# Linear-attention numerators as 64x32 tiles of TensorE, two PSUM banks a chunk, and a new table of offsets

## The chip, the cores and the metric

The kernel runs on one core of one Trainium2 chip. The metric is the device time of one execution in microseconds. Engines are named as in the profile: PE (TensorE, with PEld for its weight loads), DVE (VectorE), ACT (ScalarE), POOL (GpSimd), SP (the queue that issues DMAs).

## The reference, cut to what matters

Two attention layers are computed and laid side by side in the output. The first (A: four segments with a compressive memory) is not touched by the code of the change, only by the order of the work. The second (B) is a linear attention over 2048 tokens, 32 heads of 32 dimensions, 64 features a head:

```python
qkv = (x @ wqkv)                       # q, k, v: 32 heads of 32
pq = einsum("bhsd,hdf->bhsf", q, w_phi); pk = einsum("bhsd,hdf->bhsf", k, w_phi)
phi_q = concat([softmax(pq), softmax(-pq)]); phi_k = concat([softmax(pk), softmax(-pk)])
kv = einsum("bhsf,bhsd->bhfd", phi_k, v)      # 64 x 32 for each head
z = einsum("bhsf->bhf", phi_k)
num = einsum("bhqf,bhfd->bhqd", phi_q, kv)    # the numerators
den = einsum("bhqf,bhf->bhq", phi_q, z)[..., None] + 1e-6
out = (num / den).reshape(B, S, D) @ wo
```

## The kernel before, in words

All products run in float16 with each operand split into a high and a low half, so that a product is three matmuls: high by high, high by low, low by high (the pairs `(0, 0), (0, 1), (1, 0)` in the code).

The program is a list of operations, each with an engine, a planned duration and a priority. `Graph.run` is a planner: it walks through planned time, takes on each engine the ready operation of the smallest priority number, gives each PSUM tile one of eight banks at its first use, and emits the instructions in that order. Operations that follow one another with the same priority form a job, numbered through the program; the table `MOVES` adds an offset to the priority of a job on one engine, so a negative number draws that job's work on that engine ahead. Counted through the program, job 284 holds the last sums of `kv`, 285 the spreading of `z`, 287 the scaling and splitting of `kva` into `kls`, 291 to 298 and 303 to 310 the first two query products with their evictions (292, 294, 296, 298, 304, 306, 308 and 310 those of the evictions), 298 and 301 also the chains of the first two chunks, 299 the first projection with its stores, 340 a part of A's weights; after 390 come A's output products.

In time, the first half of the span is A's attention (to some 920 us), then B's values and states `kv` (to some 1215 us), then B's queries in 16 chunks of 128 tokens, then A's output projection (line 1666). The change lies in B's queries. Every second chunk a query product for 256 tokens is made (`strassen`, line 608, three or four banks), and `expo` (lines 1262 to 1275) makes of it the two softmaxes' exponentials `e`. For each chunk and each half `hb` of the heads POOL and DVE work out the denominators (lines 1578 to 1589) and scale `e` (line 1591), ACT and DVE split it into float16 halves `eh` (lines 1598 and 1600), and a transposing DMA on SP makes `pt`: features on partitions, two heads (2 x 64 features) in each of 8 groups (line 1603).

`kls` holds for each pair of heads a block of 128 features by 64 columns (2 heads x 32 dimensions). It is block diagonal: `bm2` has set the two quarters to zero in which one head's features meet the other's dimensions. The numerators of one half (line 1612, function `f`) are 4 x 3 x 2 = 24 matmuls over 128 partitions with 64 columns of weights and 128 tokens, two column tiles by turns, into one bank of the kind "pv". ACT then writes the high half of `ot` (line 1616) and DVE the low half (line 1618), for this half of the heads. When all of `ot` is there, `project` multiplies it by `wo` (48 matmuls of 512 columns a chunk, line 394 with `ot`), and the result goes out.

Of the kernel before, what the change touches and what calls it, by code (L numbers as in the profile page):

```python
# [12 lines left out]
AF = mybir.ActivationFunctionType  # L13
OP = mybir.AluOpType
# [5 lines left out]
D = 1024  # L20
# [34 lines left out]
         ((3, 0, "subtract"), 3, 2), ((2, 3, "subtract"), 2, 6))  # L55
EUP = 2.0 ** 15
MOVES = {
    "DVE": {
# [3 lines left out]
    "ACT": {  # L62
# [9 lines left out]
    "POOL": {  # L72
        67: 17, 70: -1, 93: -6, 131: -0.5, 141: 1, 148: -7.5, 199: 13.5, 217: -4, 238: -38, 245: 0.5, 250: -4.5, 312: -5},
    "SP": {
        88: 5.5, 89: 3.5, 134: 33.5, 149: -3.5, 226: -19.5},
}


# [20 lines left out]
class Graph:  # L99
# [84 lines left out]
    def run(self):  # L184
# [3 lines left out]
        banks, used = [[0.0, None, ()] for _ in range(8)], {k: 0 for k in self.KEEP}  # L188
        never = float("inf")
# [7 lines left out]
            if not o.wait:  # L197
                lists[o.eng].append(o)

        def bank(kind):  # L200
            rest = [x for x in banks if x[1] is None]
            if used[kind] >= self.MOST[kind] or len(rest) <= sum(
                    max(0, n - used[k]) for k, n in self.KEEP.items() if k != kind):
                return never, None
            return min((x[0], i) for i, x in enumerate(banks) if x[1] is None)

        def start(o):
            t = max(o.ready, held["POOL" if o.eng == "DVE" else "DVE"]) if o.port else o.ready
            for b in o.banks:
                if b.at is None:  # L210
                    t = max(t, bank(b.kind)[0])
            return t

        def safe(o):

            return max([o.safe] + [bank(b.kind)[0] + self.SLACK for b in o.banks if b.at is None])

        count = 0
        for _ in self.ops:
# [60 lines left out]
def tile_kernel(ctx: ExitStack, tc: tile.TileContext, ax, aw, awv, awo, beta, bx, bwqk, bwv, bphi, bwo, out):  # L280
# [93 lines left out]
    def bank(tag, shape, line=None):  # L374
        b = G.bank(tag, shape, F32, line or tag)
        psums.add(b)
        return b
# [105 lines left out]
    def rows(v, n):  # L483
        return v.rearrange("p c n -> p (c n)") if n == 1 else v.rearrange("p (a c) n -> p a (c n)", a=n)
# [1060 lines left out]
    for c in range(NT):  # L1545
# [24 lines left out]
        def otv(ot=ot):  # L1570
            return ot()[:, 0:2048].rearrange("p (a g t) -> p a g t", a=2, g=NG)

        for hb in range(2):
            e, r = er[c % 2, hb]
            dn = G.buf("b", [128, 16, 2], F32, "dn", 2)
# [21 lines left out]
            for q in range(2):  # L1597
# [5 lines left out]
            op(SP, 2.9, lambda pt=pt, hv=hv: nc.sync.dma_start_transpose(  # L1603
                pt().rearrange("p a g t -> p (a g) t"), hv().rearrange("p a n -> p (a n)")),
               r=[(eh, (hb, a, q)) for a in range(2) for q in range(2)], w=[pt], prio=P, lat=1.2, kb=64)
            pn = bank("pv", [128, 4, 128])

            def f(pn=pn, pt=pt, hb=hb):
                for g in range(4):
                    for a, b in ((0, 0), (0, 1), (1, 0)):  # L1610
                        for k in range(2):
                            nc.tensor.matmul(pn()[64 * k:64 * k + 64, g, :], kls()[:, a, 8 * hb + 2 * g + k, :], pt()[:, b, 2 * g + k, :],  # L1612
                                             start=(a + b == 0), stop=(a == 1), skip_group_check=True)

            op(PE, 0.85, f, r=[(kls, (0, hb)), (kls, (1, hb)), pt], w=[pn], prio=P)
            op(ACT, 0.55, lambda pn=pn, hb=hb, otv=otv: nc.scalar.activation(
                otv()[:, 0, 4 * hb:4 * hb + 4, :], pn(), AF.Copy, scale=2.0 ** -15), r=[pn], w=[(ot, (0, hb))], prio=P)
            op(DVE, 0.62, lambda pn=pn, hb=hb, otv=otv: nc.vector.scalar_tensor_tensor(  # L1618
                otv()[:, 1, 4 * hb:4 * hb + 4, :], pn(), 2.0 ** -15, otv()[:, 0, 4 * hb:4 * hb + 4, :], op0=OP.mult, op1=OP.subtract),
               r=[pn, (ot, (0, hb))], w=[(ot, (1, hb))], prio=P)  # L1620
        project(lambda a, g: (ot, None, lambda otv=otv: otv()[:, a, g, :]), bo, c * 128, 1024, P + 1.1)


# [114 lines left out]
```

## Time and profile before

| | |
|---|---|
| median of 3 runs | 1698.13 us (1698.09 to 1698.71) |
| the profiled execution, its own time | 1699.08 us |
| its span in the trace | 1697.4 us |
| mean granted clock of TensorE | 0.994 |
| busy: PE, DVE, ACT, POOL | 98%, 80%, 68%, 57% |
| numerators on PE (line 1612) | 768 matmuls in 32 blocks, 27.5 us busy |

The span runs from the first to the last instruction; the execution's own time has 1.7 us more around it. Busy time counts an instruction from its start to its end, and matmuls overlap, so a block's cost is read from starts, not from summed durations.

### The profile page before, as it was taken

The numbers are of one execution on the slowest core, as the hardware profiler recorded it, in microseconds if no ns is written. First come the engines' busy times: TensorE is split into PE (matmuls) and PEld (weight loads), VectorE is DVE, ScalarE is ACT, GpSimd is POOL, SyncE is SP. The second block draws the span as 40 slices with busy tenths as digits, with TensorE's granted clock in tenths as the row PEclk, the third lists the DMA queues.
The fourth block names the chain that finished last, engine by engine and source line by source line (L and its number), as shares of the span: only waits on it lengthen the run. The fifth ranks groups of instructions, "written<-read, shape, count | busy, mean of one in ns | idle before, by whom it ended". The sixth has DMA issues, their size and how long they took to land.

```text
span 1697.4 us, 38668 instructions
## 1 busy us (share of the span) xinstructions
PE 1668.2 (98%) x14408; PEld 1002.5 (59%) x14408; DVE 1354.2 (80%) x3205; ACT 1158.9 (68%) x2131; POOL 965.4 (57%) x1280
## 2 busy tenths in 40 slices
PE   8999999999999999999999999999999999999999
PEld 6677676766767767767765455445544444444444
DVE  5889998899988869698895779677998887975441
ACT  8788899878879797868675477765545644544331
POOL 3346588554468885848552577645488887640000
PEclk8999999999999999999999999999999999999999
DMA  5556465755776665764467465467645876773311
GB/s 192 165 183 176 139 206 175 242 160 163 225 179 204 184 173 150 199 189 131 95 182 266 156 224 162 137 194 278 224 94 149 199 162 174 214 168 129 124 62 62
DMA packets 261933, 292.47 MB, mean 172 GB/s; under 512 B 138865, under 2 KB 192881, under 8 KB 255089
## 3 DMA queue, kind: packets, MB, share of 16 engines
q1 hardware_dynamic: 261744, 290.01, 57.3%
q8 instruction: 113, 1.85, 0.5%
q14 instruction: 76, 0.61, 0.1%
HBM read 161.17 MB, written 86.05 MB: 146 GB/s over the span
## 4 chain that ended last, share of the span: by engine, by line
PE 45%; DVE 5%; DMA 1%; ACT 0%; issue 0%; SPq 0%; DVEq 0%; ACTq 0%
PE proj L608 17%; PE misc L394 8%; PE proj L1666 5%; PE s L608 4%; PE s L1666 2%; PE misc L608 2%; PE kv L1423 1%; PE misc L1666 1%; PE pv L1612 1%; DVE S L1600 1%; PE proj L394 1%; DVE mx L1262 1%; DVE r L1272 1%; DVE dn L1581 1%; PE pv L1007 1%; PE s L971 1%
## 5 line engine op out<-in xcount | busy, mean ns | idle before, releaser
L394 PE MATMUL proj<-S,S 128*128 128x128 f16 (+1 forms) x3072 | 508.8, 301 | 4.1 <-ACT S L427 1.7
L394 PEld LDWEIGHTS <-S 128*128 128x128 f16 x4608 | 330.2, 98 | 152.0 <-issue 13.0
L608 PE MATMUL proj<-S,S 128*128 128x512 f16 x1584 | 364.6, 379 | 2.4 <-ACT cs L614 2.4
L608 PEld LDWEIGHTS <-S 128*128 128x128 f16 x2016 | 191.9, 98 | 220.5 <-issue 3.3
L984 POOL TENSOR_SCALAR_AFFINE_SELECT ph<-ph 128x256 f16<-128x256 f16 (+1 forms) x448 | 195.8, 458 | 155.2 <-DVE ph L978 136.7
L876 DVE CUSTOM_DVE_ANT_0 s<-s,causal 128x512 f32<-128x512 f32 (+3 forms) x512 | 242.9, 509 | 15.2 <-PE s L870 11.5
L978 DVE SCALAR_TENSOR_TENSOR ph<-s,ph 128x512 f16<-128x512 f32 x320 | 210.2, 683 | 36.8 <-ACT ph L977 35.3
L977 ACT ACTIVATE ph<-s 128x512 f16<-128x512 f32 x320 | 189.9, 653 | 1.0 <-PE pv L1007 0.2
L394 PE MATMUL misc<-S,ot 128*128 128x512 f16 x768 | 170.8, 379 | 1.8 <-DVE ot L1618 1.8
L1269 ACT ACTIVATE e<-e,sk 128x256 f32<-128x256 f32 x256 | 113.3, 497 | 63.7 <-DVE e L1266 58.2
L394 PEld LDWEIGHTS <-ot 128*128 128x128 f16 x768 | 73.8, 98 | 90.3 <-DVE ot L1618 2.2
L971 PE MATMUL s<-S 104*128 104x512 f16 (+3 forms) x512 | 114.4, 299 | 1.9 <-ACT S L898 0.8
L870 PE MATMUL s<-S 96*128 96x512 f16 (+3 forms) x512 | 112.8, 299 | 2.1 <-DVE mt L876 1.4
L975 ACT ACTIVATE s<-s,os 128x512 f32<-128x512 f32 x160 | 106.5, 707 | 9.0 <-PE s L971 8.5
L975 ACT ACTIVATE s<-s,bd 128x512 f32<-128x512 f32 x160 | 106.6, 712 | 7.1 <-PE s L971 6.5
L1578 POOL TENSOR_TENSOR e<-e,zb 128x512 f32<-128x512 f32 x64 | 87.2, 1376 | 30.4 <-DVE r L1272 25.6
L394 PE MATMUL proj<-wv,S 128*128 128x128 f16 x1536 | 103.0, 219 | 0.0
L1007 PEld LDWEIGHTS <-ph 128*128 128x128 f16 x2560 | 87.1, 96 | 15.5 <-issue 0.8
L1272 DVE TENSOR_REDUCE r<-e 128x32 f32<-128x1024 f32 x64 | 76.9, 1208 | 24.2 <-ACT e L1269 24.2
L1007 PE MATMUL pv<-vl,ph 128*128 128x66 f16 (+1 forms) x2560 | 91.9, 184 | 0.5 <-DVE h L824 0.3
L876 DVE DVE_READ_ACCUMULATOR2_ANT mt<- 128x1 f32 x512 | 72.4, 141 | 0.0
L1011 DVE TENSOR_REDUCE oall<-pv 128x132 f32<-128x264 f32 x128 | 54.5, 426 | 19.1 <-PE pv L1007 18.5
(334 smaller groups left out, 3268.8 us busy)
## 6 DMA issues: line engine op xcount, KB each, us to landing
S<-xf_d SPq DMA_DIRECT2D x126, 256.0 KB
S<-h SPq DMA_DIRECT2D x192, 128.0 KB
S<-wf_d SPq DMA_DIRECT2D x21, 1024.0 KB
st<-bwqk SPq DMA_DIRECT2D x64, 256.0 KB
out<-os SPq DMA_DIRECT2D x40, 256.0 KB
S<-aw SPq DMA_DIRECT2D x16, 512.0 KB
wa_d<-S SPq DMA_DIRECT2D x16, 512.0 KB
wf_d<-fo SPq DMA_DIRECT2D x32, 256.0 KB
```

The source lines that it names most:

```text
L394: op(PE, dur, lambda c=c, a=a, b=b, lv=lv, rv=rv: nc.tensor.matmul(pv(), lv(), rv(), start=(c == 0 and a + b == 0), stop=(c == n - 1 and a ...
L608: op(PE, 0.215, lambda n=n, a=a, b=b, lv=lv, rv=rv: nc.tensor.matmul(ps(), lv(), rv(), start=(start and n == 0 and a + b == 0), stop=(n == ...
L870: nc.tensor.matmul(ps()[:, o:o + 128 * i + 128], st()[0:96, 0, h, 128 * i:128 * i + 128], st()[0:96, 1, h, 0:128 * i + 128], start=True, s ...
L876: dve(0.12 + 0.00113 * n, lambda h=h, i=i, o=o, n=n: nc.vector.tensor_tensor_reduce(ps()[:, o:o + n], ps()[:, o:o + n], causal[:, 512 - n: ...
L971: nc.tensor.matmul(ps()[:, o:o + n], st()[0:104, 1, h, 128 * j:128 * j + 128], st()[0:104, 0, h, 128 * j:512], start=True, stop=True)
L975: act(0.59, lambda: nc.scalar.activation(ps(), ps(), AF.Exp, bias=0.0, scale=bdv()[:, 3, i2, 0:1]), r=[(bd, i2)], w=[ps])
L977: act(0.5, lambda: nc.scalar.activation(ph()[:, 0], ps(), AF.Copy, scale=2.0 ** 14), r=[ps], w=[(ph, 0)])
L978: dve(0.6, lambda: nc.vector.scalar_tensor_tensor(ph()[:, 1], ps(), 2.0 ** 14, ph()[:, 0], op0=OP.mult, op1=OP.subtract), r=[ps, (ph, 0)], ...
L984: nc.gpsimd.affine_select(pd, pd, pattern=[[0, n], [1, 128]], compare_op=OP.is_ge, fill=0.0, base=0, channel_multiplier=-1)
L1007: nc.tensor.matmul(ps()[:, i, n0:n1], ph()[:, a, o:o + 128], vl()[:, j, h, n0:n1], start=(i == 0 and a == 0), stop=(j == min(i, 2)), skip_ ...
L1269: op(ACT, 0.41, lambda i=i: nc.scalar.activation(e()[:, 4 * i:4 * i + 4], e()[:, 4 * i:4 * i + 4], AF.Exp, bias=0.0, scale=sk()[:, i:i + 1 ...
L1666: op(PE, 0.215, lambda n=n, a=a, b=b: nc.tensor.matmul(ps(), v(a)[:, n, :], wform[w]()[:, b, n, :], start=(start and n == 0 and a + b == 0 ...
```

## The change

A block of numerators now multiplies only the two quarters of `kls` that are not zero: 48 matmuls over 64 partitions with 32 columns of weights and 128 tokens. Neighbours in the order fall into eight tiles of the array: two halves of the rows (`h`) by four quarters of the columns (`k`). The two row halves write into two banks, `pn[0]` of kind "pv" and `pn[1]` of kind "kv", which both halves `hb` of a chunk fill before they are evicted. So ACT and DVE evict twice a chunk as before, but after both blocks, and each eviction writes four groups of `ot` that lie two apart. The rows of `wo` are permuted on the way in to fit. The planner can now open two banks for one operation (`opening`), and its duration for a block goes from 0.85 to 0.5. The table `MOVES` is another on all five engines.

```diff
 MOVES = {
...
     "DVE": {
-        43: -0.5, 70: 1, 85: -12.5, 88: -6, 93: -8, 101: -5.5, 103: 11, 106: -2, 109: 2, 114: -3.5, 118: 3.5, 129: -6, 135: -5,
-        139: -16.5, 141: 6, 148: 4, 158: 21, 183: -3, 199: -6, 217: -3, 219: 7.5, 238: -53, 245: 5, 250: -16.5, 266: -1.5,
-        282: -3.5, 306: 22, 318: 3, 360: 5},
+        53: 0.5, 70: 1.5, 85: -19.5, 88: -7, 89: 0.6, 93: -16.5, 96: -3.5, 101: -5.5, 103: 11, 104: -1, 106: -5, 109: 3,
+        114: -10.5, 118: 4.5, 126: 1.5, 133: 0.5, 139: -15.5, 141: 5.5, 148: 5.5, 152: 1.5, 158: -1, 178: -4.5, 179: -1.5,
+        183: -3.5, 202: 0.6, 209: -5.5, 217: -4, 219: 8, 238: -46.5, 250: -21.5, 257: -3, 270: 3, 282: -11.5, 284: -135,
+        287: -83, 292: -88.5, 293: -90, 298: -256, 301: -245, 306: -166, 318: 7, 360: 5.5, 367: -1, 378: -4, 383: -3.5},
...
     "PE": {
...
+        261: -8, 270: -6, 272: 1, 274: -2, 276: -1, 282: -5, 284: -115.5, 293: -2, 297: -4.5, 299: 2.5, 309: -8, 317: -3,
+        319: -57.5, 321: 0.5, 330: 4.5, 335: -4.5, 341: 2.5, 351: 11.5, 357: 3.5, 363: -7, 367: 3, 373: 9.5},
     "SP": {
-        88: 5.5, 89: 3.5, 134: 33.5, 149: -3.5, 226: -19.5},
+        88: 4.5, 89: 4, 188: 14.5, 299: -9.5, 340: -10.5},
...
+        def opening(o):
+            kinds = [b.kind for b in o.banks if b.at is None]
+            return [bank(k, kinds[:i]) for i, k in enumerate(kinds)]
...
+        pn = [bank(k, [128, 4, 128], "sums") for k in ("pv", "kv")]
         for hb in range(2):
...
-            pn = bank("pv", [128, 4, 128])
-
             def f(pn=pn, pt=pt, hb=hb):
-                for g in range(4):
+                for n in range(2):
                     for a, b in ((0, 0), (0, 1), (1, 0)):
-                        for k in range(2):
-                            nc.tensor.matmul(pn()[64 * k:64 * k + 64, g, :], kls()[:, a, 8 * hb + 2 * g + k, :], pt()[:, b, 2 * g + k, :],
-                                             start=(a + b == 0), stop=(a == 1), skip_group_check=True)
-
-            op(PE, 0.85, f, r=[(kls, (0, hb)), (kls, (1, hb)), pt], w=[pn], prio=P)
-            op(ACT, 0.55, lambda pn=pn, hb=hb, otv=otv: nc.scalar.activation(
-                otv()[:, 0, 4 * hb:4 * hb + 4, :], pn(), AF.Copy, scale=2.0 ** -15), r=[pn], w=[(ot, (0, hb))], prio=P)
-            op(DVE, 0.62, lambda pn=pn, hb=hb, otv=otv: nc.vector.scalar_tensor_tensor(
-                otv()[:, 1, 4 * hb:4 * hb + 4, :], pn(), 2.0 ** -15, otv()[:, 0, 4 * hb:4 * hb + 4, :], op0=OP.mult, op1=OP.subtract),
-               r=[pn, (ot, (0, hb))], w=[(ot, (1, hb))], prio=P)
+                        for k in range(4):
+                            for h in range(2):
+                                i, rows_ = 4 * n + k, slice(64 * h, 64 * h + 64)
+                                nc.tensor.matmul(pn[h]()[32 * k:32 * k + 32, 2 * hb + n, :],
+                                                 kls()[rows_, a, 8 * hb + i, 32 * h:32 * h + 32], pt()[rows_, b, i, :],
+                                                 start=(a + b == 0), stop=(a == 1), skip_group_check=True)
+
+            op(PE, 0.5, f, r=[(kls, (0, hb)), (kls, (1, hb)), pt], w=pn, prio=P)
+        for h in range(2):
+            def oh(a, h=h, otv=otv):
+                return otv()[:, a].rearrange("p (g h) t -> p h g t", h=2)[:, h]
+
+            op(ACT, 0.55, lambda pn=pn, h=h, oh=oh: nc.scalar.activation(oh(0), pn[h](), AF.Copy, scale=2.0 ** -15),
+               r=[pn[h]], w=[(ot, (0, h))], prio=P)
+            op(DVE, 0.62, lambda pn=pn, h=h, oh=oh: nc.vector.scalar_tensor_tensor(
+                oh(1), pn[h](), 2.0 ** -15, oh(0), op0=OP.mult, op1=OP.subtract),
+               r=[pn[h], (ot, (0, h))], w=[(ot, (1, h))], prio=P)
...
-        "bwo": rows(B_wo),
+        "bwo": rows(np.asarray(B_wo).reshape(4, 4, 2, 32, D).transpose(0, 2, 1, 3, 4).reshape(D, D)),
```

## Rows read from the trace of the kernel before

**Rows 1.** The page: busy time, share of the span, instructions.

```profile
PE 1668.2 (98%) x14408; PEld 1002.5 (59%) x14408; DVE 1354.2 (80%) x3205; ACT 1158.9 (68%) x2131; POOL 965.4 (57%) x1280
```

**Rows 2.** Busy time by stretch; the columns stand in the first line.

```profile
core 0: us, PE busy (x) PEld busy (x) DVE busy (x) ACT busy (x) POOL busy (x), PEclk, DMA share, GB/s
...
100.00:1200.00 1100.00, 1091.66 (x10679) 707.82 (x10678) 923.99 (x2403) 854.46 (x1583) 691.77 (x963) 1.00 0.60 184
1200.00:1300.00 100.00, 91.79 (x667) 46.31 (x666) 95.62 (x161) 52.87 (x105) 70.78 (x70) 1.00 0.59 161
1300.00:1530.00 230.00, 229.52 (x1541) 109.10 (x1540) 192.10 (x320) 119.49 (x228) 165.74 (x177) 1.00 0.71 179
```

**Rows 3.** The chain that ended last, from 1288 us: start, us, what.

```profile
1288.56 5.03 DVE S L1600 x3
1293.59 0.26 DVE r L1275
1293.85 0.56 DVE ot L1618
...
1294.85 0.79 PE pv L1612 x24
...
1528.04 0.79 PE pv L1612 x24
1528.83 19.53 PE misc L394 x90
1548.36 2.59 PE proj L1666 x12
```

**Rows 4.** Line 1612: durations in ns (least, median, most), first and last start.

```profile
L1612 PEld LDWEIGHTS <-kls x768: 106/110/110, 1245.4 to 1528.6; 128*64 128x64 f16 x192
L1612 PE MATMUL pv<-pt,kls x768: 219/219/243, 1245.4 to 1528.6; 128*64 128x128 f16 x192
```

**Rows 5.** Instructions in order of time around one block (start, us): PE, then PEld.

```profile
1297.52 0.81 PE L394 MATMUL misc<-S,ot 128*128 128x512 f16 x3
1298.26 0.86 PE L1612 MATMUL pv<-pt,kls 128*64 128x128 f16 x24
1299.06 0.39 PE L394 MATMUL misc<-S,ot 128*128 128x512 f16 x1
...
1298.26 0.70 PEld L1612 LDWEIGHTS <-kls 128*64 128x64 f16 x24 [0.42 <-DMA pt<-S]
```

**Rows 6.** Line 1612 alone, in short windows; (x) counts running instructions.

```profile
core 0: us, PE busy (x) PEld busy (x), PEclk, DMA share, GB/s
1298.25:1298.27 0.02, 0.01 (x2) 0.01 (x2) 1.00 0.17 51
1298.28:1298.34 0.06, 0.06 (x2) 0.06 (x4) 1.00 0.02 0
1298.34:1298.36 0.02, 0.02 (x4) 0.02 (x6) 1.00 0.00 0
```

**Rows 7.** Line 896, loads of 8 columns: durations in ns.

```profile
L896 PEld LDWEIGHTS <-mh x128: 82/86/87, 58.1 to 896.6; 128*8 128x8 f16 x128
```

**Rows 8.** Instructions in order of time on PE around line 1007.

```profile
494.58 0.73 PE L1007 MATMUL pv<-vl,ph 128*128 128x66 f16 x20
495.15 1.67 PE L394 MATMUL proj<-S,S 128*128 128x512 f16 x7
```

**Rows 9.** Groups by line: 1300 to 1530 us, the last row 1200 to 1300.

```profile
L1600 DVE TENSOR_TENSOR S<-e,S 128x512 f16<-128x512 f32 x48 | 45.6, 995 | 3.1 <-ACT S L1598 2.9
L1618 DVE SCALAR_TENSOR_TENSOR ot<-pv,ot 128x512 f16<-128x512 f32 x25 | 16.9, 675 | 6.2 <-ACT ot L1616 6.2
L1616 ACT ACTIVATE ot<-pv 128x512 f16<-128x512 f32 x25 | 14.8, 591 | 14.1 <-PE pv L1612 14.0
...
L1600 DVE TENSOR_TENSOR S<-e,S 128x512 f16<-128x512 f32 x16 | 20.3, 1325 | 0.0
```

**Rows 10.** What PE waited for, 1200 to 1530 us: total, times, longest.

```profile
PE pv L1612 <- DMA pt<-S: 3.0, 3, 1.5
...
PE misc L394 <- DVE ot L1618: 1.8, 1, 1.8
```

More of the change, by code (lines that the diff above doesn't have):

```diff
@@ L57 @@
 MOVES = {
-    "DVE": {
[3 rows of a table removed]
-    "ACT": {
[9 rows of a table removed]
-    "POOL": {
-        67: 17, 70: -1, 93: -6, 131: -0.5, 141: 1, 148: -7.5, 199: 13.5, 217: -4, 238: -38, 245: 0.5, 250: -4.5, 312: -5},
+    "ACT": {
[4 rows of a table added]
+    "DVE": {
[4 rows of a table added]
+    "POOL": {
[8 rows of a table added]
     "SP": {
-        88: 5.5, 89: 3.5, 134: 33.5, 149: -3.5, 226: -19.5},
[1 row of a table added]
 }
@@ L198, in run, with bank @@
                 lists[o.eng].append(o)
-        def bank(kind):
-            rest = [x for x in banks if x[1] is None]
+        def bank(kind, before=()):
+            rest = sorted(x[0] for x in banks if x[1] is None)[len(before):]
             if used[kind] >= self.MOST[kind] or len(rest) <= sum(
-                    max(0, n - used[k]) for k, n in self.KEEP.items() if k != kind):
-                return never, None
-            return min((x[0], i) for i, x in enumerate(banks) if x[1] is None)
+                    max(0, n - used[k] - (k in before)) for k, n in self.KEEP.items() if k != kind):
+                return never
+            return rest[0]
+        def opening(o):
+            kinds = [b.kind for b in o.banks if b.at is None]
+            return [bank(k, kinds[:i]) for i, k in enumerate(kinds)]
         def start(o):
             t = max(o.ready, held["POOL" if o.eng == "DVE" else "DVE"]) if o.port else o.ready
[L209 to L212, printed above, removed]
+            return max([t] + opening(o))
         def safe(o):
-            return max([o.safe] + [bank(b.kind)[0] + self.SLACK for b in o.banks if b.at is None])
+            return max([o.safe] + [t + self.SLACK for t in opening(o)])
         count = 0
```

17 rows, old and new, of the table MOVES are left out of this document.

## The prediction

> **What bounds the kernel now.** I read the page's busy shares first: TensorE is busy 98% of the span, VectorE 80% [rows 1]. A share is a mean, so the next view is the busy time by stretch [rows 2]. The numerators run from 1245 to 1529 us [rows 4], that is in the third and fourth stretch. From 1300 to 1530 TensorE is idle for 230.00 - 229.52 = 0.5 us: whatever TensorE saves there should come off the end. From 1200 to 1300 it is idle for 8.2 us while VectorE is busy 95.6 of 100 us: there VectorE sets the pace, and TensorE's savings are worth nothing by themselves. The chain of waits says the same and gives the border [rows 3]: it runs through VectorE (the splits of line 1600, then an eviction of line 1618) until 1294, and from 1294.85 through TensorE to the end, with all 25 numerator blocks from 1294.85 to 1528.04 on it. The other 32 - 25 = 7 lie before the border. The granted clock is 1.00 in all these stretches [rows 2], the upper of its two levels (2.4 GHz), so nothing is to be had from it there.
>
> **The numerator block, before.** A block (one of the 32 calls of `f`) is 24 matmuls of 128x128 in two column tiles, each with its own load of 64 columns [rows 4]. What it costs is read from the stream around it [rows 5]: three projection matmuls start at 1297.52, one takes 2.59 / 12 = 0.216 us of the stream [rows 3], so the next would have started at 1298.17. The block's first matmul starts at 1298.26 (0.09 us of entry), its last ends 0.86 us later and lasts 0.22, so first to last start is 0.64 us, and the next projection starts at 1299.06, 0.16 us after the last start. The block costs 1299.06 - 1298.17 = 0.89 us. Inside [rows 6]: two loads and two matmuls have started by 1298.27, no more matmuls until 1298.34, then two more at once. So the two column tiles run side by side, in rounds: 12 rounds, the first 0.08 us long, the others (0.64 - 0.08) / 10 = 0.056.
>
> **The same block, after.** 48 matmuls with half the rows and half the columns, each with a load of 32 columns, ordered so that eight neighbours lie in eight different tiles (two row halves, each in a bank of its own, by four column quarters). If eight run side by side as two do now, there are 6 rounds: 0.08 + 4 x 0.056 = 0.30 us from the first to the last round. Four instructions start within 0.02 us in rows 6; sixteen for a round within some 0.03 to 0.06, which fits a round of 0.056; I add 0.03 for the last round's spread. With the same entry and exit (0.89 - 0.64 = 0.25) the block costs 0.58 us: 0.31 less.
>
> No row shows row tiles or four column tiles at once, so I bound the price. From below: 0.25 + 0.30 = 0.55, a saving of 0.34. From above, the nearest rows of closely packed work: 20 matmuls of 66 and 33 columns with loads of 128 columns start at 494.58 and leave the stream at 495.15 [rows 8], 0.57 / 20 = 28.5 ns for a load with its matmul. At that price 48 cost 1.37 us and the block 1.62, 0.73 more than now. I take the value near the lower end, since rows 6 show this very line's loads and matmuls starting in pairs, which that 28.5 ns as a limit on every start would not allow.
>
> Here the Trainium skill speaks against the change ("TensorE: Matmul & The Clock Gate", section on the 56 ns gap): matmuls never start less than about 25 ns apart. Rows 6 disagree as far as tiles go, since two start inside 20 ns, twice. By the rule 48 matmuls would take 1.2 us, and 25 blocks would add some 14 us to the sum.
>
> The loads get a bound of their own. A load of 64 columns lasts 110 ns [rows 4], one of 8 columns 86 [rows 7], so a column adds 24 / 56 = 0.43 ns and 32 columns occupy 13.7 ns. Were all 48 loads to queue behind one another, that is 48 x 13.7 = 0.66 us, what the 24 matmuls take now: the gain of the block would be nothing.
>
> **Evictions.** Two a chunk before, two after, of 128x512 elements each: ScalarE 0.59 us, VectorE 0.68 [rows 9]; the count and size stay, and only the order of the written groups changes, so I price them at no change. But both now wait for the second half of the heads. The chunk's `ot` is whole after ScalarE, VectorE, VectorE (0.59 + 0.68 + 0.68) where before it was ScalarE and VectorE after the second half: 0.68 us later. The projection of a chunk needs all of `ot` already before, so nothing is newly ordered; the cover is the projection of the chunk before: after the last numerators 90 projection matmuls follow [rows 3], 48 of them the last chunk's own, so 42 x 0.216 = 9.1 us lie between. I cost it at nothing; without the cover it would be 16 x 0.68 = 10.9 us. TensorE takes its list in order, so a block that waits for its two banks holds up the projections and query products queued behind it, and these in turn the evictions that feed VectorE. One chunk holds both banks from its first half's block to its last eviction, so the next chunk's first block is the one that would wait; TensorE's waits of that kind are now 3.0 us on `pt` and 1.8 on an eviction, in 330 us [rows 10].
>
> **The table of offsets.** It reorders all engines from job 43 on. What it moves most is VectorE around the border: the last sums, the scaling of `kva` and the first query evictions (jobs 284 to 306) get -83 to -256, which draws them ahead of everything that VectorE has, where the old table had only +22 on job 306. That is the stretch with 8.2 us of TensorE idle. The displaced work is the exponentials and splits of later chunks, needed anyway in the same stretch, and a split costs 1.3 us there against 1.0 later [rows 9], so not all can come back. Bounds: 8.2 us back, or as much lost again. I take a third back, 2.7 us, which includes the 7 blocks before the border. From 100 to 1200 us there are 1100 - 1091.66 = 8.3 us idle; the small offsets there could give back at most these or lose as much, and no row favours a sign: 0. SP's queue has two moves in this stage, job 299 (two stores of `out`) and job 340 (weights), both forward; TensorE waits 3.0 us in all for the transposed `pt` that goes through the same queue [rows 10], which bounds what they can spoil or mend: 0. The permuted rows of `bwo` move no bytes more.
>
> **Sum.** The profiled execution took 1699.08 us, 0.95 above the median of 1698.13. 1699.08 - 25 x 0.31 (7.75) - 2.7 = 1688.6, and on the median's footing 1687.7. A difference under about 0.2% (3.4 us) can't be told from none.
>
> **Rivals.**
> - *One pair at a time* (slower): the array takes a load and its matmul no faster than rows 8 show. Place: the 25 blocks on the chain. Price 25 x 0.73 = 18 us, so 1698.1 + 18 - 2.7 = 1714. It decides from 0.64 / 47 = 13.6 ns between starts, where the block costs what it does now; I forecast 0.33 / 47 = 7 ns. For it: no two starts of untiled matmuls in rows 8 are closer. Against it: rows 6. Chance 0.08.
> - *Loads queue* (nothing gained by the block): 0.66 us as above; then only the table is left, 1698.1 - 2.7 = 1695.4. For it: 24 loads of 64 columns at 0.43 ns are 0.66 us, which is also what the block takes. Against it: 110 ns loads that start in pairs. Chance 0.12. The Trainium skill (same page, section on LDWEIGHTS) prices a load at its columns over 1.2 GHz, 27 ns for 32 columns. Laid end to end, today's 24 loads of 64 columns would take 1.28 us by it; the trace has 0.70 from the first's start to the last's end [rows 5], so they don't queue across column tiles. Row tiles it doesn't show.
> - *The evictions or the table hurt*: both banks of a chunk wait behind a burst of splits such as the 5.03 us of rows 3, and the 0.68 us is uncovered in each chunk: 1698.1 - 7.75 + 10.9 = 1701. For it: an eviction that came 1.8 us late already [rows 10]. Against it: VectorE is idle 230 - 192 = 38 us in the fourth stretch [rows 2]. Chance 0.09.
> - *More comes back*: all 32 blocks count (9.9 us) with the 8.2 us and part of the 8.3: below 1680. Chance 0.07.
> - *The forecast*: 1680 to 1694. Chance 0.64.
>
> **How the numbers follow.** The time is the forecast's, 1687.7. The range runs from 1678, which takes in the upper part of "more comes back", to 1699, which takes in "loads queue" and the edge of late evictions: 0.64 + 0.03 + 0.12 + 0.02 = 0.81. Faster by 0.2% (under 1694.7): 0.64 + 0.07 + 0.05 of "loads queue" = 0.76. Within: 0.07 + 0.04 = 0.11. Slower (over 1701.5): 0.08 + 0.05 = 0.13.
>
> **What would show it.** The block: 48 matmuls whose first to last start is near 0.33 us, with the next line's matmul 0.16 us behind; eight starts inside 0.06 us. If that stretch is 0.64 or more, the loads or the starts are the limit. The border: idle TensorE time from 1200 to 1300 under 8.2 us, and the chain entering TensorE before 1294. The evictions: waits of TensorE on line 1618's successor staying near 2 us. The prediction is wrong if the block is as forecast and the time isn't: then look for TensorE idle time between 1300 and 1530, or in the attention stages, whose order the table changed too.

## The result and the profile after

The changed kernel is slower: 1701.66 us median of 20 runs (1698.49 to 1704.69) against 1696.75 of 20 (1694.38 to 1699.43), a ratio of 1.0027 with a 95% interval of [1.0021, 1.0033], some 4.6 us. The prediction, 1687.7 in a range of 1678 to 1699, had the wrong sign. The two profiled executions hide this: both took 1699.1 us at a mean granted clock of 0.994. They lost it in different places. The one of before ran at half clock for a part of its first 100 us (0.90 there, after 0.98); the one of after lost clock at the border of the query stage. So the stage itself is to be compared: from the first numerators to A's output projection it was 1548.36 - 1245.4 = 303.0 us before [rows 3, 4] and is 1548.35 - 1243.3 = 305.1 now, although its TensorE work has become 8 us less. The clock differs over all runs as well: the mean granted clock of after's 20 executions is 0.989 to 0.995 (median 0.993), that of 92 executions of before, taken in the sessions of the experiments, 0.993 to 1.000 (median 0.997).

The page and the busy time by stretch, after (columns as in [rows 1] and [rows 2]):

```profile
PE 1658.5 (98%) x15176; PEld 993.2 (59%) x15176; DVE 1356.0 (80%) x3205; ACT 1157.7 (68%) x2131; POOL 968.0 (57%) x1280
```

```profile
0.00:100.00 100.00, 90.25 (x791) 64.06 (x792) 77.99 (x238) 79.12 (x136) 39.88 (x76) 0.98 0.60 187
100.00:1200.00 1100.00, 1092.47 (x10685) 708.55 (x10683) 923.92 (x2394) 853.21 (x1582) 695.05 (x960) 1.00 0.60 184
1200.00:1300.00 100.00, 86.47 (x778) 41.94 (x777) 94.76 (x163) 53.20 (x106) 72.40 (x75) 0.93 0.57 156
1300.00:1530.00 230.00, 225.87 (x2172) 104.76 (x2171) 187.81 (x308) 113.62 (x219) 160.66 (x171) 1.00 0.69 172
...
1240.00:1260.00 20.00, 13.04 (x140) 5.39 (x138) 19.04 (x30) 6.94 (x15) 12.84 (x16) 0.74 0.60 121
1290.00:1297.00 7.00, 4.64 (x60) 2.02 (x61) 5.05 (x10) 4.45 (x11) 6.08 (x9) 0.76 0.91 237
```

The first 100 us of before, the same view:

```profile
0.00:100.00 100.00, 91.82 (x769) 65.42 (x770) 73.96 (x224) 76.53 (x133) 37.12 (x72) 0.90 0.57 181
```

TensorE's busy time fell by 9.7 us. But from 1300 to 1530 its idle time rose from 0.5 to 4.1 us, and from 1200 to 1300 from 8.2 to 13.5: 9.0 us more idle for some 8 us less work. The clock row fell from 1.00 to 0.93 between 1200 and 1300; the two short stretches show where (0.74 and 0.76, a mix of the levels 2.4 and 1.2 GHz).

The block's line (now 1617) by durations, and one block in order of time, after:

```profile
L1617 PEld LDWEIGHTS <-kls x1536: 88/89/148, 1243.3 to 1529.2; 64*32 64x32 f16 x192
L1617 PE MATMUL pv<-pt,kls x768: 212/216/312, 1243.3 to 1529.2; 64*32 64x128 f16 x192
L1617 PE MATMUL kv<-pt,kls x768: 213/223/311, 1243.3 to 1529.2; 64*32 64x128 f16 x192
```

```profile
1299.34 3.19 PE L398 MATMUL misc<-S,ot 128*128 128x512 f16 x14
1302.45 0.23 PE L1617 MATMUL pv<-pt,kls 64*32 64x128 f16 x1
...
1302.47 0.23 PE L1617 MATMUL kv<-pt,kls 64*32 64x128 f16 x1
1302.52 0.22 PE L1617 MATMUL pv<-pt,kls 64*32 64x128 f16 x1
...
1302.83 0.22 PE L1617 MATMUL kv<-pt,kls 64*32 64x128 f16 x1
1302.98 2.27 PEld L398 LDWEIGHTS <-ot 128*128 128x128 f16 x12
```

Fourteen projections from 1299.34 would hand over at 1299.34 + 14 x 0.216 = 1302.36; the next projection starts at 1302.98. So this block costs 0.62 us. First to last start is 0.38 us, entry 0.09, exit 0.15. Eight matmuls, one for each tile, start within 0.02 us, then the next eight 0.07 later. In nearly all blocks first to last start is 0.36 to 0.38 us, where it was 0.64: 0.26 us a block, so 32 x 0.26 = 8.3 us saved, an estimate. The order of after with the old tiles (among the experiments) bears it out: TensorE is busy 1666.6 us there and 1658.5 in after, 8.1 less.

What TensorE waited for from 1200 to 1530 us, and pieces of the chain that ended last, after:

```profile
PE pv L1617 <- DMA pt<-S: 9.1, 6, 2.9
PE pv L1617 <- DVE kls L1476: 2.9, 1, 2.9
...
PE kv L1617 <- DVE ot L1628: 0.4, 1, 0.4
```

```profile
1236.04 4.92 DVE S L1605 x4
...
1247.48 1.92 DVE kls L1476
...
1286.96 5.35 DMA pt<-S
...
1370.99 9.45 DMA pt<-S x2
...
1426.19 6.06 DMA pt<-S
...
1514.03 4.89 DMA pt<-S
...
1529.47 18.89 PE misc L398 x87
1548.35 2.59 PE proj L1676 x12
```

Before, the chain entered TensorE at 1294.85 and from there to the end left it once, in the part that [rows 3] leave out. The chain, and what TensorE waited for from 1294 to 1530 us, before:

```profile
1314.12 1.50 PE proj L608 x7
1315.62 5.87 DMA pt<-S
...
1321.54 0.86 PE pv L1612 x24
```

```profile
PE pv L1612 <- DMA pt<-S: 0.5, 1, 0.5
```

So a `pt` for which TensorE waited only 0.5 us already stood on the path. (The chain hands over to this DMA from a query product on TensorE; by the code it needs the splits, and VectorE's last ones end at 1315.45, 0.17 us before it starts.) Now the chain keeps leaving TensorE: in these rows alone three times after 1300, each time for the transposing DMA that makes `pt`, and before that for VectorE too (the splits are now line 1605). The wait for `pt` is 9.1 us where it was 3.0 [rows 10].

### The profile page after: what moved, and what is told of

Read it like the earlier page. It is cut to its first block, busy times and chain, and to the rows that moved or that the text cites. A ratio compares the mean times of both kernels' runs of the same rounds, so it can differ in the third digit from the quotient of the medians.

```text
span 1697.4 us, 40207 instructions
## 1 busy us (share of the span) xinstructions
PE 1658.5 (98%) x15176; PEld 993.2 (59%) x15176; DVE 1356.0 (80%) x3205; ACT 1157.7 (68%) x2131; POOL 968.0 (57%) x1280
## 4 chain that ended last, share of the span: by engine, by line
PE 60%; DVE 10%; ACT 3%; DMA 3%; issue 1%; SPq 0%; POOL 0%; ACTq 0%; DVEq 0%
PE proj L612 14%; PE proj L398 14%; PE misc L398 7%; PE proj L1676 5%; PE s L612 3%; PE s L1676 2%; PE s L975 2%; PE pv L1011 2%; DMA pt<-S 2%; PE s L874 2%; PE misc L612 2%; DVE S L1605 2%; DVE s L880 2%; PE misc L1676 1%; DVE mx L1266 1%
## 5 line engine op out<-in xcount | busy, mean ns | idle before, releaser
L398 PE MATMUL proj<-S,S 128*128 128x512 f16 (+1 forms) x3072 | 504.6, 299 | 5.0 <-DVE S L433 2.0
L398 PE MATMUL misc<-S,ot 128*128 128x512 f16 x768 | 174.6, 385 | 0.7 <-ACT ot L1626 0.7
L1605 DVE TENSOR_TENSOR S<-e,S 128x512 f16<-128x512 f32 x64 | 68.2, 1107 | 11.6 <-ACT S L1603 11.6
```

The lines of the kernel that those rows point to most:

```text
L398: op(PE, dur, lambda c=c, a=a, b=b, lv=lv, rv=rv: nc.tensor.matmul(pv(), lv(), rv(), start=(c == 0 and a + b == 0), stop=(c == n - 1 and a ...
```

## The experiments

Three explanations for the lost gain are held against one another. The feeder: splits and transposing DMA are nearly as late as TensorE, so time saved on TensorE turns into waiting for `pt`. The banks: two of the eight banks held until a late eviction make TensorE, which works in order, wait elsewhere. The table: the new order is itself the worse one. Each ratio is to the kernel before, run beside it, with its 95% interval in brackets.

**Old structure, less work on TensorE.** The block keeps 128x64 tiles and the order of before, and leaves out one of its three products (the diff) or two (only `(0, 0)` stays).

```diff
-                    for a, b in ((0, 0), (0, 1), (1, 0)):
+                    for a, b in ((0, 0), (0, 1)):
...
-                                             start=(a + b == 0), stop=(a == 1), skip_group_check=True)
+                                             start=(a + b == 0), stop=(b == 1), skip_group_check=True)
```

> The kernel of before with the low-by-high products of the numerators left out: 16 matmuls of 24 in a block, everything else and the order as before. It prices TensorE time in this stage: a block gets 8 x 27.8 ns = 0.22 us shorter, 7.1 us over 32. If late evictions are what cancels the change's saving: 5 to 7 us under before, 1688 to 1690. If the chain of pt is the bound: under 2 us, 1693 to 1696.

> As the one with 16 of 24, but only the high-by-high products of the numerators: 8 matmuls, 0.445 us less a block, 14.2 us over 32. If TensorE time in this stage comes off the end: 10 to 14 us under before, 1681 to 1685. If the chain of pt takes over as the bound: 2 us or less, and TensorE waits on pt grow from 3 us to 12 or more.

16 of 24: 1692.19 us, 0.9987 [0.9978, 0.9996]. 8 of 24: 1685.55 us, 0.9943 [0.9930, 0.9955]. Four rounds of 0.056 us in 32 blocks are 7.2 us, eight are 14.3. Only 2.2 us of the first (0.13% of 1695.4) and 9.7 of the second come off the end. Waits of TensorE, 1200 to 1530, with 8 of 24:

```profile
PE pv L1612 <- DMA pt<-S: 6.5, 8, 1.6
PE proj L608 <- ACT cs L614: 2.9, 3, 1.6
```

With no edit of banks, evictions or table, the wait for `pt` more than doubles (3.0 before). So time taken off TensorE does turn into waiting, but the feeder is not a wall. Its share is smaller than what is lost: idle time from 1200 to 1530 grew by 1.9 us with 16 of 24 and 3.7 with 8 of 24, while 5.0 and 4.6 us did not come off the end (by the intervals 3.5 to 6.5 and 2.4 to 6.7). With 16 of 24 the clock row from 1200 to 1300 was 0.98; with 8 of 24 it was 1.00.

**Evictions and banks.** First, old tiles and table, but a chunk's two banks held to the end and then evicted:

```diff
+        pn = [bank(k, [128, 4, 128], "sums") for k in ("pv", "kv")]
...
-            op(PE, 0.85, f, r=[(kls, (0, hb)), (kls, (1, hb)), pt], w=[pn], prio=P)
+            op(PE, 0.85, f, r=[(kls, (0, hb)), (kls, (1, hb)), pt] + ([pn[0]] if hb else []), w=[pn[hb]], prio=P)
+        for hb in range(2):
...
-                otv()[:, 0, 4 * hb:4 * hb + 4, :], pn(), AF.Copy, scale=2.0 ** -15), r=[pn], w=[(ot, (0, hb))], prio=P)
+                otv()[:, 0, 4 * hb:4 * hb + 4, :], pn[hb](), AF.Copy, scale=2.0 ** -15), r=[pn[0], pn[1]], w=[(ot, (0, hb))], prio=P)
```

> The kernel of before with its 128x64 tiles, table and durations, but a chunk's two halves in two banks that are both evicted only after the second half's block. If late evictions and held banks cost time: 3 us or more over before (1700 and up). If the order or the chain of pt is at fault: within 2 us of before, 1695 to 1699.

1700.03 us, 1.0032 [1.0020, 1.0044]: about 5.4 us lost, by a part of the change that had been priced at nothing. Its chain shows where:

```profile
1286.68 6.25 DVE S L1601 x4
1292.94 0.61 DVE ot L1618
1293.55 0.04 issue
1293.59 0.38 PE proj L608
```

```profile
PE proj L608 <- DVE ot L1618: 3.3, 1, 3.3
```

An eviction sits behind a burst of four splits on VectorE (6.25 us). TensorE's next query product needs the bank that it would free, and everything behind that product waits 3.3 us. Then the second bank alone: every engine's order is that of before, replayed instruction by instruction, the tiles too, and a second bank is opened and released with the first but not used.

```diff
-            pn = bank("pv", [128, 4, 128])
+            pn = [bank(k, [128, 4, 128], "sums" if k == "kv" else None) for k in ("pv", "kv")]
...
-            op(PE, 0.85, f, r=[(kls, (0, hb)), (kls, (1, hb)), pt], w=[pn], prio=P)
+            op(PE, 0.85, f, r=[(kls, (0, hb)), (kls, (1, hb)), pt], w=pn, prio=P)
```

> The kernel of before in exactly its order, 128x64 tiles and one eviction a half, but each block also takes a second bank that is held until the eviction and not used. If the second bank is what cancels the small tiles' saving in the same order (TensorE waits to open a bank that the numerators still hold): 3 to 6 us over before, 1698 to 1702, with TensorE waits of 4 us or more on the VectorE eviction. If the split evictions or the pt chain cancel it: as before within 2 us.

1698.38 us, 1.0019 [1.0008, 1.0029], and TensorE's row of this kind:

```profile
PE proj L630 <- DVE ot L1643: 2.5, 1, 2.5
```

Holding a second bank costs some 3 us by itself. The cause within the run stays open: besides this wait the clock is lower at the border (0.97 in its row from 1200 to 1300), and TensorE's idle time from 1200 to 1530 is 9.0 us where before had 8.7, since other waits are gone.

**Small tiles without the new table.** Three kernels take the table of before: the tiles and late evictions of after with the old planned duration (0.85 for 0.5); the same with evictions after each half, four small ones of 128x256; and small tiles with the order of before replayed on all engines, again evicted after each half. One piece of each diff, the first two against after, the third against before:

```diff
-            op(PE, 0.5, f, r=[(kls, (0, hb)), (kls, (1, hb)), pt], w=pn, prio=P)
+            op(PE, 0.85, f, r=[(kls, (0, hb)), (kls, (1, hb)), pt], w=pn, prio=P)
...
-                                nc.tensor.matmul(pn[h]()[32 * k:32 * k + 32, 2 * hb + n, :],
+                                nc.tensor.matmul(pn[h]()[32 * k:32 * k + 32, n, :],
...
-            o = min(some, key=lambda x: x.prio)
...
+            else:
+                o = order[count]
```

> As the first, but the planner goes on counting 0.85 us for a block, so that the order stays nearly that of before and only the blocks on the chip are shorter. Order at fault: the full saving of the 25 to 32 blocks, 1688.5 to 1690.5. Chain of pt at fault: within 2 us of before, 1695 to 1699. Late evictions at fault: 1697 or more.

> Small tiles, table of before, 0.85 us planned for a block, but two banks for each half, each evicted right after that half's block (four evictions of 256 columns an engine and chunk, planned at 0.275 and 0.31 us). If the late evictions cancel the blocks' saving: 5 to 8 us under before, 1687 to 1690, ratio 0.995 to 0.997, and no TensorE wait of 2 us or more that names the VectorE eviction. If the chain of pt bounds the queries: as before within 2 us, 1693 to 1697. If the extra fixed cost of the split evictions (some 32 more on VectorE and on ScalarE) bites: over 1697.

> Small tiles and two banks for each half, evicted early, in exactly the order of before on every engine (the planner first makes the order as if there were one bank, then it is replayed); each eviction is two instructions of 256 columns. If TensorE time in this stage passes through as in the run with 16 of 24 matmuls (3.2 of 7.1 us): 1691 to 1693. If the saving passes in full, 1687 to 1689. If the small tiles themselves bring nothing (or the split evictions cost as much): 1694 to 1697.

1.0000 [0.9991, 1.0010], 1.0004 [0.9995, 1.0014] and 0.9998 [0.9990, 1.0007]: nothing gained in any. With the early evictions of the second kernel no wait for an eviction is over 1.0 us, and the wait for `pt` stands in their place:

```profile
PE pv L1615 <- DMA pt<-S: 8.3, 6, 2.5
```

The replay is the cleanest of all these runs, since only tiles, the second bank and the split evictions differ:

```profile
PE pv L1637 <- DMA pt<-S: 5.9, 5, 2.5
PE proj L630 <- DVE ot L1651: 3.9, 1, 3.9
PE kv L1637 <- DVE ot L1651: 2.2, 2, 1.2
```

```profile
1200.00:1300.00 100.00, 87.58 (x840) 43.04 (x839) 95.05 (x164) 54.50 (x115) 70.11 (x70) 0.98 0.58 159
1300.00:1530.00 230.00, 226.60 (x2131) 104.98 (x2129) 191.89 (x342) 119.67 (x249) 163.14 (x176) 1.00 0.73 180
```

TensorE is idle for 15.8 us where before had 8.7: 7.1 of the 8.3 us saved came back as waits for `pt` and for banks. A cure was tried on it: a planner that avoids banks just left by numerators.

```diff
-                    b.at = min((any(mine.get(d.eng, 0) < d.place for d in x[2] if d.eng != e), x[0], i)
+                    b.at = min((any(mine.get(d.eng, 0) < d.place for d in x[2] if d.eng != e), x[0] + 6.0 * (not b.num and x[3]), i)
```

> Small tiles in exactly the order of before, as in the ninth run, but other tiles take a bank that numerators have just left only if no other has been free for some time. If opening such a bank is what TensorE waits for: the waits on the VectorE eviction fall from 6.1 us to 2 or less and the time to 1690 to 1693. If the chain of pt bounds: 1694 to 1697, with pt waits over 6 us.

1.0018 [1.0007, 1.0029], and the waits for evictions stayed (3.9 and 2.5 us). A miss: this rule removed no wait. That the number of banks held is part of the cause rests on the run with the second bank, not on this one.

**The table and the order.** Old tiles with the new table; old tiles with only its offsets from job 238 on; old tiles in exactly after's order, with its banks and late evictions; and after with the low half of `kls` drawn ahead in a replay of its order. The diffs, in this order (of the tables one engine's part, the others go likewise):

```diff
-        88: 5.5, 89: 3.5, 134: 33.5, 149: -3.5, 226: -19.5},
+        88: 4.5, 89: 4, 188: 14.5, 299: -9.5, 340: -10.5},
```

```diff
-        88: 5.5, 89: 3.5, 134: 33.5, 149: -3.5, 226: -19.5},
+        88: 5.5, 89: 3.5, 134: 33.5, 149: -3.5, 226: -19.5, 299: -9.5, 340: -10.5},
```

```diff
-                                nc.tensor.matmul(pn[h]()[32 * k:32 * k + 32, 2 * hb + n, :],
-                                                 kls()[rows_, a, 8 * hb + i, 32 * h:32 * h + 32], pt()[rows_, b, i, :],
...
+                            nc.tensor.matmul(pn[hb]()[64 * k:64 * k + 64, g, :], kls()[:, a, 8 * hb + 2 * g + k, :], pt()[:, b, 2 * g + k, :],
```

```diff
+        n = max(at[d] for d, _ in self.ahead.deps) + 1
+        order.remove(self.ahead)
+        order.insert(n, self.ahead)
...
-        op(DVE, 0.62, lambda hb=hb, v=v: nc.vector.tensor_tensor(kls()[:, 1, v], kva[hb](), kls()[:, 0, v], op=OP.subtract),
+        G.ahead = op(DVE, 0.62, lambda hb=hb, v=v: nc.vector.tensor_tensor(kls()[:, 1, v], kva[hb](), kls()[:, 0, v], op=OP.subtract),
```

> 128x64 tiles, one bank a half and the planner's 0.85, with the new table. If the new table's order is at fault: slower than the changed kernel, 1705 to 1710 (1701.7 and some of the 8.3 us of the blocks). If the chain that makes pt is the bound: between before and after, 1697 to 1702, since the larger blocks only fill idle time. If the late evictions are at fault: as before, 1697.

> The other half: old offsets before job 238, new ones from 238 on, with the tiles of before. If the new table's cost lies in the queries: 1698 to 1701, with a wait of the first numerators on kls of 3 us or more. If it lies in the attention stages: as before within 2 us.

> The changed kernel in exactly its own order, with its two held banks, late evictions and table, but with the 24 matmuls of 128x64 in each block. If the changed order leaves TensorE waiting anyway, so that the blocks' 8.3 us are lost in it: 1700 to 1703, as the changed kernel. If the blocks' saving is in the changed kernel's time and the order costs more than it: 1705 to 1710.

> The changed kernel in exactly its order but for one VectorE instruction: the low half of kls for the second heads, which stands at 1247 us, is put right behind the ScalarE copy that it needs. If the order of the new table around the border is at fault there: the wait on kls (2.9 us) goes, and with it some of the 10 us at half clock that begin at 1245: 3 to 6 us under the changed kernel, 1696 to 1699. If the numerators then wait for pt as long: 1700 to 1703.

1.0030 [1.0019, 1.0040]; 1.0051 [1.0039, 1.0063]; 1.0052 [1.0040, 1.0064]; 1.0024 [1.0015, 1.0033]. The table costs where it was thought to give. The first run's time lies where its expectation put the chain of `pt`, but its trace names another wait, the one on `kls` at the border, while the wait for `pt` is 3.1 us, as before:

```profile
PE pv L1615 <- DVE kls L1475: 3.9, 1, 3.9
```

The second run came out slower than any of its cases and without that wait; like the partial tables below it is an order of its own and prices no part. The third says what the tiles are worth in the change as it stands: 1.0052 - 1.0027 = 0.25%, 4.2 us of the 8.3 (some 2 to 6.5 by the two intervals); the rest of the change, table and late evictions together, costs 0.52%, 8.8 us. How much of that is the table's no replay separates. How part of it arises can be read at the border, after:

```profile
1246.92 1.91 POOL L1596 TENSOR_TENSOR e<-e,r 128x1024 f32<-128x1024 f32 x1
1247.40 1.98 DVE L1476 TENSOR_TENSOR kls<-ez,kls 128x512 f16<-128x512 f32 x1
1249.43 0.36 PEld L1617 LDWEIGHTS <-kls 64*32 64x32 f16 x32 [3.17 <-DVE kls L1476]
```

The new offsets bring the first chunk's splits forward, but leave the low half of `kls` behind them: it starts at 1247.4 (before at 1227.7), and the first chunk's second block stands in its middle for 2.9 us. Drawing it ahead removed that wait, though not the time beyond doubt (the intervals overlap): the waits for `pt` (8.5 us) and the lower clock (0.93) stayed.

**Partial tables.** After with the table of before (and the new planned duration 0.5); after without its seven VectorE offsets from 284 to 306; old tiles with only the new offsets below job 238.

```diff
-        88: 4.5, 89: 4, 188: 14.5, 299: -9.5, 340: -10.5},
+        88: 5.5, 89: 3.5, 134: 33.5, 149: -3.5, 226: -19.5},
```

```diff
-        183: -3.5, 202: 0.6, 209: -5.5, 217: -4, 219: 8, 238: -46.5, 250: -21.5, 257: -3, 270: 3, 282: -11.5, 284: -135,
-        287: -83, 292: -88.5, 293: -90, 298: -256, 301: -245, 306: -166, 318: 7, 360: 5.5, 367: -1, 378: -4, 383: -3.5},
+        183: -3.5, 202: 0.6, 209: -5.5, 217: -4, 219: 8, 238: -46.5, 250: -21.5, 257: -3, 270: 3, 282: -11.5, 318: 7,
+        360: 5.5, 367: -1, 378: -4, 383: -3.5},
```

```diff
-        88: 5.5, 89: 3.5, 134: 33.5, 149: -3.5, 226: -19.5},
+        88: 4.5, 89: 4, 188: 14.5},
```

> Small tiles, two banks and the planner's 0.5 for a block, with the table of before. If the new table's order is at fault (TensorE then waits for pt), the 32 x 0.26 us = 8.3 us that the blocks save come through: about 1689, ratio 0.995, TensorE idle from 1200 to 1530 near the 8.7 us of before. If the chain that makes pt (POOL, ScalarE, VectorE, transposing DMA) bounds the queries whatever the order, the saving turns into idle time: within 2 us of before, idle near 17. If the late evictions and the two held banks are at fault: 1697 to 1702, with TensorE waits that name line 1626 or 1628.

> The changed kernel without the seven VectorE offsets of jobs 284 to 306 (-83 to -256). If these offsets open the idle time of TensorE between 1240 and 1255 us (the first numerators wait for kls and pt there, and the clock falls to half): 3 us or more under the changed kernel, 1693 to 1697. If not: 1698 or more; an order that fits the planned times worse can also make it much slower, as in the first run.

> The kernel of before with the new offsets for the jobs before 238 (attention) and the old ones from 238 on. If the new table's cost lies in the queries (idle TensorE around 1245 us): as before within 2 us, 1693 to 1697. If it lies in the attention stages: 1698 or more.

1.0154 [1.0135, 1.0172], 1.0177 [1.0163, 1.0192], 1.0158 [1.0145, 1.0171]. Each is 26 to 30 us slower, outside every case of the first expectation; the other two had named 1698 or more. The likely reason is that the planner, given one other duration or a part of a table, falls into an order that no one tuned; where these orders lose their time was not followed up. They tell how brittle the order is, and nothing of what a single part is worth; the replays come nearer to that.

**The account.** For each kernel whose queries lie in the same stretch: TensorE time saved in the blocks; idle time from 1200 to 1530 (330 us less its busy time) over the 8.7 of before; the clock's loss, (1 - clock row) x length of the two stretches; their sum; and the measured change (ratio - 1, times before's median). All in us.

| kernel | saved | idle | clock | sum | measured |
|---|---|---|---|---|---|
| after | -8.3 | +9.0 | +7.0 | +7.7 | +4.6 |
| after, `kls` ahead | -8.3 | +6.2 | +7.0 | +4.9 | +4.1 |
| small tiles, order of before | -8.3 | +7.1 | +2.0 | +0.8 | -0.3 |
| the same, banks rested | -8.3 | +8.1 | +2.0 | +1.8 | +3.1 |
| small tiles, old plan | -8.3 | +3.2 | +5.3 | +0.2 | 0.0 |
| the same, early evictions | -8.3 | +5.5 | +2.3 | -0.5 | +0.7 |
| old tiles, 16 of 24 | -7.2 | +1.9 | +2.0 | -3.3 | -2.2 |
| old tiles, 8 of 24 | -14.3 | +3.7 | 0 | -10.6 | -9.7 |
| old tiles, late evictions | 0 | +3.8 | 0 | +3.8 | +5.4 |
| old tiles, second bank held | 0 | +0.3 | +3.0 | +3.3 | +3.2 |
| old tiles, new table | 0 | +1.3 | +5.0 | +6.3 | +5.1 |
| old tiles, late offsets | 0 | +3.8 | +3.0 | +6.8 | +8.6 |
| old tiles, order of after | 0 | +3.8 | +7.0 | +10.8 | +8.8 |

One profile stands for each kernel, slowed work that covers a wait is counted as loss, and a clock row is read to a hundredth, which is 1.0 us in the one stretch and 2.3 in the other; so the sum is rough. It follows the measured change to 3.1 us for after and to 2.0 or less for the other twelve. By this account the blocks' saving on TensorE is taken back by idle time and clock.

## Why the prediction was wrong

- **The block**: right in its mechanism, the size a little off. Six rounds of eight tiles, 0.38 us from first to last start instead of 0.33, entry and exit unchanged; 0.26 us a block instead of 0.31, since the last two rounds spread to some 10 ns between starts. "One pair at a time" and "loads queue" are refuted: 48 loads and matmuls start in 0.38 us, 0.38 / 47 = 8 ns apart, and 48 loads one behind another would have taken 0.66. The Trainium skill ("TensorE: Matmul & The Clock Gate", section on the 56 ns gap) has matmuls never start less than some 25 ns apart; with eight tiles the trace shows 8 ns, so the rule doesn't hold across tiles.
- **"Whatever TensorE saves there should come off the end"** is the step that failed first. 0.5 us of idle time says that the feeder was hardly late before; it doesn't say by how much it was early. The rows were at hand. The chain does not run "from 1294.85 through TensorE to the end": 5.87 us of it, from 1315.62, are the DMA that makes `pt`, so what TensorE saves ahead of it comes off the end only as far as that DMA comes earlier too. And the wait for `pt`, 3.0 us in three places [rows 10], was used as a bound on what SP's moves could do, and not read as a feeder with no slack there. The runs with 16 and 8 of 24 matmuls show what the sentence was worth: 2.2 of 7.2 us, 9.7 of 14.3.
- **The sizes**: from the forecast, 10.4 us under before, to the result, 4.6 over, it is 15 us. The blocks hold 3.5 of them (-7.75 forecast, -4.2 measured in after's order). The larger part, 11.5, is the table and the evictions: -2.7 forecast, +8.8 measured for both together.
- **Evictions "at nothing"** failed as well. The cover named, the projection of the chunk before, is real for `ot`'s reader, and no projection (`misc`) waited more than 2.2 us for an eviction in any of the runs (1.8 before, 0.7 after). What was missed is who else waits for a bank: a query product (`proj`), which needs several and holds up what follows it in TensorE's order (3.3 us with late evictions, 3.9 in the replay). The prediction had the sentence (a block that waits holds up what is queued behind it) but looked for it in the blocks alone; they waited too, though less (2.2 us in the replay, 0.4 in after). Late evictions cost 0.32%, a second bank alone 0.19%. The Trainium skill ("TensorEngine Tiling (Array Packing)", Gotcha 1) says that different row tiles cannot access one PSUM bank at the same time; so by it the second bank is part of the price of row tiles. No run here put both row halves into one bank.
- **The table**, put at -2.7 us within bounds of -8.2 and +8.2, costs 0.30% in the old structure, for which it was not tuned. The border lost what it was to gain: 8.2 us of idle time became 13.5, and the granted clock 0.93. The argument (seven jobs are drawn ahead, so TensorE starts earlier) was true of the start (1243.3 instead of 1245.4), and missed that job 287, with the low half of `kls` in it, is drawn ahead by less (-83) than the first two chunks' chains (-256 and -245): that half came 20 us later than before.
- **The rival** that came true is "the evictions or the table hurt", 1701 at a chance of 0.09, with its place (banks behind a burst of splits) but not its mechanism of 0.68 us in each chunk: where a bank is waited for, it is one or two waits of 2.5 to 4 us. In after itself that wait is only 0.4 us; with its table and planned duration the waits are for `pt` and `kls`. That its 1701 is the measured time is luck: the price was 16 x 0.68 us, which no run shows.
- **Left open**: how much of after's 4.6 us is the clock, as no run held the order and changed the clock alone. The executions give a hint: at a mean granted clock of 0.994 eight of after's average 1700.3 us and three of before's 1698.7, so that at an equal clock some 1.6 us remain; and the kernels with the new late offsets (but for the partial tables) have a median clock of 0.993 or 0.994 in their executions, the others 0.995 to 0.998. Whether the lower clock makes the waits longer or the waits lower the clock isn't shown. Open too: why the late-eviction kernel kept a clock of 1.00 through a 3.3 us wait at 1290, where after fell to half; and which of the late offsets costs most. No version tried that computes the whole beat the kernel before.

## What to carry to other kernels

An engine that is 98% busy with half a microsecond idle is the bound only until its work shrinks: before counting a saving in full, ask how early its feeder is, read the chain piece by piece, and if it or the row of waits already names the feeder, count a part. When a change holds a scarce buffer longer, look for the instruction that opens most of such buffers at once on an in-order engine, not for the one that reads the data. An order tuned on planned durations belongs to the kernel it was tuned for: test a new tile in the replayed old order, and the new order with the old tile, before believing either.

## What the hardware showed that was not expected

- Eight tiles of 64x32 start within 0.02 us of one another, each with its own load of 89 ns; entry into and exit from a block are 0.09 and 0.15 us as for two tiles of 128x64 (0.09 and 0.16).
- A VectorE subtraction of 128x512 took 1.98 us beside a POOL operation of 1.91 us that had started 0.5 us earlier; the same instruction for the first heads took 0.68 us at 1219.7.
- Twice in after's query stage the granted clock fell to 1.2 GHz (0.50 from 1246 to 1254) while TensorE, at 2.4 GHz and mostly busy until then (36.3 us of the 40 from 1200, 29.5 of the 30 from 1260), had waits of 1 to 3 us (20 us from 1240: 13.0 busy, 0.74; 7 us from 1290: 4.6 busy, 0.76). At the upper level before, the same first stretch was 17.8 us busy.
